# One queue less in front of the decays: loads of a recurrent attention, moved to another engine and to a later slot

## The chip, the cores and the metric

The program runs on one core of a Trainium2 chip. The metric is the device time of one execution in microseconds (us). The core has TensorE (PE: matrix products), VectorE (DVE), ScalarE (ACT), GpSimd (POOL) and SyncE (SP), each of which works through its own instructions in order. Transfers are issued by an instruction on one of these engines and are then carried out by 16 shared DMA engines; an instruction that needs a transfer's data waits on a semaphore. A queue in this text is the row of instructions of one engine, with the transfers that it issues.

## The reference, cut to what matters

Three stages follow each other: a recurrent attention (4 batches, 8 heads, 768 steps, head size 40), a mixture of experts with top-1 gating, and a second network with an ELU.

```python
for t in range(S):
    y[:, :, t] = np.einsum('bhd,bhde->bhe', rt, state)
    Sa = np.einsum('bhde,bhe->bhd', state, at)
    state_decay = state * wt[:, :, None, :] - np.einsum('bhd,bhe->bhde', Sa, bt)
    state = state_decay + np.einsum('bhd,bhe->bhde', vt, kt)
...
out[i] = gate_w[i] * y[expert_idx[i], pos[i]]      # per token: one of 8 experts, relu in between
...
return (g @ w_out).astype(np.float32)              # g = elu(x @ w_in)
```

## The kernel before, in words

The 768 steps are cut into 12 chunks of 64, and each chunk into two halves of the batch and head pairs: 24 units, each of 64 steps for 16 pairs. A chunk is computed with products instead of a loop over steps. For each unit the kernel needs the decays (with `a`, `k` and `b` in the same array, `e_in`), from which VectorE makes running products (`pre_dve`, L227 on); score matrices between steps (`scores`, L259); the inverse of a triangular 64x64 matrix per pair; and then a short serial part that uses the state that the unit two before has left (`rhs`, `u_solve`, `vu_tr`, `s_update`, `y_mm`, `x_out`).

The inverse is made in three steps. The scores of a unit are stored to DRAM (`dab`, L278) and loaded again in another layout (`lm_load`, L308). GpSimd then inverts all 32x32 diagonal blocks of a group of four units in one long row of small operations (`solve`, L319) and stores the result to DRAM (`dx`, `x_store`, L342). `tt_load` (L354) loads a unit's share of it into `TA` and `TT`, and `t64` (L409) joins the 32x32 blocks to 64x64: first a transpose on VectorE (L413), then products on TensorE (L420, L431). Groups of four start at units 4, 8, 12, 16 and 20 (units 0 to 3 have two groups of two).

The order of all work is written out by hand. A long string, `ORDER`, sets the beginning. From slot 5 to slot 24, `slot(k)` (L53) writes a slot's steps as a string of keys, and each key runs one step, up to its next `yield`. In slot k the serial part of unit k runs beside the preparation of unit k + 8 (its scores) and k + 9 (its running products), so that a slot has work of several units. The letters that matter here: `c` scores, `m` their mask, `l` the load of scores for the solve, `i` a third of a solve, `o` the store of its result, `e` the load of the decays, `d` the load of `r` and `v` (`RVU`), `v` a load for `rhs` (`VS`), `t` the load of an inverse, `g` joining it, `r` the product `rhs` with which a slot begins on TensorE, `w` the transposes of `VU`, `p` and `a` the running products and copies made from the decays.

All loads and stores named above are issued by SyncE, in program order, except most stores of `dx` and the scattered rows of the output, which GpSimd issues. A transfer that has to wait, for its source or for its buffer, holds SyncE's queue until it can go. The decays have two buffers (`EI`, in tiles called `ring`): those of unit u + 2 overwrite those of unit u, once unit u's scores and transposed keys (`kb_tr`, L286) are made. From slot 14 on there are no decays left to load, and from slot 17 on VectorE also converts weights for the last stage.

Of the kernel before, what the change touches and what calls it, by code (L numbers as in the profile page):

```python
# [22 lines left out]
NU = 24  # L23
LOOK = 8

FU, KMU = 4, 8
GROUPS = [(u, 2) for u in range(0, FU, 2)] + [(u, 4) for u in range(FU, NU, 4)]
# [17 lines left out]
h4 x2 l8 g4 c12.1 k12.0 D1 h4 t5 q3.0 p13 w3 g4 g4 g4 s3 u4 x2 a13 l12 s3 z3 q3.0 u4 w4 w4 a13 q3.1 p13 i3 w4 g5 h5 y3  # L45
d5 x2 w4 y3 s3 s4 i3 k12.0 e14 t6 s4 s4 h5
"""
AHEAD = (17, 19, 20, 21, 22, 23)

CV0, CVN = 17, 7  # L50
# [2 lines left out]
def slot(k):  # L53
    L = []
    a = lambda x: L.extend(x.split())
    live, prev = k < NU, k >= 1
    nx, up = k + 1, k + 8
    ups = up < NU
    pair = k - 3 if k >= 3 and k % 2 else None
    work = {f - 5 + i: (g, i) for g, (f, n) in enumerate(GROUPS) for i in range(3) if n == 4 and f > 4}  # L60
    w = work.get(k)
    if k + 2 < NU: a(f"v{k+2}")
    if live: a(f"r{k} r{k}")
    if ups: a(f"c{up}.0")
    if FU <= k < NU: a(f"g{k} g{k}")
    if ups: a(f"m{up}.0 c{up}.0")
    more = ups and up + 1 < NU
    if more: a(f"p{up+1}")
    if k < 2: a(f"c{up}.1 m{up}.1 c{up}.1 c{up}.1 l{up}")
    if k == 1: a(f"q{k-1}.0 q{k-1}.0 q{k-1}.1 q{k-1}.1")  # L70
    if k >= 2: a(f"x{k-2} x{k-2} x{k-2}")
    if k == NU: a(f"b{NU-2}.1")
    if FU <= k < NU: a(f"g{k} g{k}")
    if w and w[1]:
        a(f"i{w[0]}")
        if w[1] == 2: a(f"o{w[0]}")
    if k >= 4 and k % 2 == 0: a(f"D{k-3}")
    if ups and k > 1:
        a(f"c{up}.1 m{up}.1 c{up}.1 c{up}.1")
        if more: a(f"p{up+1}")  # L80
        a(f"l{up}")
    V = (lambda: a("V")) if CV0 <= k < NU else (lambda: None)
    if k > 1: a(f"q{k-1}.0 q{k-1}.0")
    V()
    if w and not w[1]: a(f"i{w[0]}")
    if live: a(f"u{k} u{k}")
    if more: a(f"p{up+1}")
    if k > 1: a(f"q{k-1}.1 q{k-1}.1")
    V()
    if 2 <= nx < NU: a(f"h{nx} h{nx}")  # L90
    if pair is not None: a(f"b{pair}")
    if ups:
        a(f"k{up}.0 k{up}.0 k{up}.1 k{up}.1")
        if up + 2 < NU: a(f"e{up+2}")
    if FU <= nx < NU: a(f"g{nx}")
    if live and k < 22: a(f"w{k} w{k} w{k} w{k}")
    if more: a(f"a{up+1} a{up+1}")
    if prev and k > 2: a(f"z{k-1}")
    if nx < NU: a(f"d{nx}")
    if k + 2 < NU: a(f"t{k+2}")  # L100
    if live and k < 22: a(f"s{k} s{k} s{k}")
    if k == NU: a(f"j{NU-2}.1 j{NU-2}.1 D{NU-2}")
    if prev: a(f"y{k-1} y{k-1}")
    V()
    if pair is not None: a(f"j{pair} j{pair} D{pair}")
    return " ".join(L)


def attention(tc, nc, e_in, v_tok, d_in, wg, disp, cst, ring, early, cv, cap):
# [8 lines left out]
    def bank(nm):  # L118
        return ps.tile([128, 512], F32, tag="ps", name=nm)
# [90 lines left out]
    def q64(t):  # L210
        return t.rearrange("p (q t) -> p q t", t=65)[:, :, 0:64]

    def load_e(u, half=None):
        c = slice(0, 2058) if half is None else slice(1034 * half, 1034 + 1024 * half)
        t = EI[u % 2]
        for hp in range(2):
            nc.sync.dma_start(out=t[64 * hp:64 * hp + 40, c], in_=e_in[u, hp, :, c])

    def load_v(u):
        VS = VSs[u % 3]  # L220
# [286 lines left out]
    def q_mm(u, g):  # L507
        V, R = VUt[u % 2], Rbd[u % 2]
        p = bank("q")
        for i in range(4):  # L510
            h = 4 * g + i
            nc.tensor.matmul(p[:, 128 * i:128 * i + 128], V[:, h].rearrange("p x t -> p (x t)"), R[:, h], start=True, stop=True)  # L512
        yield
        if ("Qs", u) not in st:
            st["Qs", u] = wk.tile([128, 8, 2, 64], F32, tag="Qs", name="Qs", bufs=1)
        Qs, m = st["Qs", u], mask.unsqueeze(1).to_broadcast([128, 8, 64])
        nc.vector.tensor_tensor(Qs[:, 4 * g:4 * g + 4].rearrange("p h b t -> p (h b) t"), p.rearrange("p (l t) -> p l t", t=64), m, op=ALU.mult)
# [86 lines left out]
    def zero_d(e):  # L604
        zero(disp[e * NTOK:e * NTOK + 512, :])

    steps = dict(sz=set_z, se=set_e, sa=set_a, sd=set_d, sv=set_v, st=set_t, sr=set_r, ss=set_s, sx=set_x, sw=set_w, sc=set_c, lw=load_w,
                 e=load_e, v=load_v, d=load_d, p=pre_dve, a=pre_act, c=scores, m=am_evac, k=kb_tr, l=lm_load, i=solve, o=x_store,
                 n=m_load, t=tt_load, f=t32, g=t64, r=rhs, u=u_solve, w=vu_tr, s=s_update, h=s_tr, q=q_mm, z=y_state, y=y_mm, x=x_out,
                 b=route, j=route_mm, D=scatter, Z=zero_d, V=lambda: cv.pieces(spare, CVN))  # L610

# [12 lines left out]
    def go(key):  # L624

        if key not in open_:
            nm = key.rstrip("0123456789.")
            args = map(int, key[len(nm):].split(".")) if nm != key else ()
            open_[key] = part(steps[nm], args)
        next(open_[key], None)  # L630
# [10 lines left out]
    for k in range(KR, NU + 1):  # L641
        for key in slot(k).split():
            go(key)
        for _ in range(AHEAD.count(k)):
            next(early, None)
        if 8 <= k < 14:
            i = k - 8
            zero(cst["yd"][4096 + 512 * i:4608 + 512 * i, :])
# [65 lines left out]
class Ring:  # L714
# [8 lines left out]
    def next(s, split):  # L723
        k = s.turn[split]
        s.turn[split] += 1
        return [s.tile(i, F32R) for i in ((1, 2), (4, 5), (6, 7), (8, 9))[k % 4]] if split else s.tile((0, 3)[k % 2], F32)
# [505 lines left out]
def network(tc, nc, e_in, v_tok, d_in, wg, cap, w1, w2, w_in, w_out, out):  # L1232
    with tc.tile_pool(name="cst", bufs=1) as p, tc.tile_pool(name="dsp", bufs=1, space=DRAM) as dp, tc.manual_schedule():
        cst = consts(p)
        disp = dp.tile([8 * NTOK, D], F32, name="disp")
        cst["yd"] = dp.tile([4096 + NTOK, D], F32, name="yd")
        ring = Ring(p)
        w32 = dp.tile([4, 128, 2816], F32, name="w32")
        W0, cv = expert(nc, ring, w1, w2, 0), Convert(nc, w_in, w_out, w32)
        attention(tc, nc, e_in, v_tok, d_in, wg, disp, cst, ring, ahead(W0), cv, cap)  # L1240
        ffn(tc, nc, cst, disp, w1, w2, w32, out, ring, W0, cv)
# [26 lines left out]
```

## Time and profile before

| | us |
|---|---|
| median of 3 runs | 1132.35 (1128.07 to 1134.58) |
| the profiled execution | 1126.71 |
| its span, first to last instruction | 1125.0 |
| TensorE busy in it | 996.1 (89%) |
| VectorE busy | 739.7 (66%) |
| GpSimd busy | 575.2 (51%) |
| ScalarE busy | 500.3 (44%) |

The attention takes up to about 464 us of the span, the two networks the rest. Times in rows are counted from the start of the span, so that a row at 213.58 lies in the attention. Slots are named by the k of `slot(k)`; in the profile slot 7 begins at 194.62 us, slot 8 at 207.89 and slot 20 at 393.0, each time with the `rhs` product. The mean granted TensorE clock over the whole span is 0.922 of full speed.

### The profile page before, as it was taken

Reading aid. Unit: us, or ns where it says so; the run is one execution under the profiler, and the core shown is the slowest. Engines: PE = TensorE matmul, PEld = TensorE weight load, DVE = VectorE, ACT = ScalarE, POOL = GpSimd, SP = SyncE. Lnnn points to the kernel's source line nnn. Section 1 sums busy time; section 2 is a strip of 40 time slices with the busy share of each in tenths; the row PEclk is TensorE's granted clock in tenths of the full one; section 3 lists DMA queues with packets and bytes.
Section 4 is the critical chain, followed back from the end, with each engine's and each line's share of the span. In section 5 each row is a group of like instructions: output and inputs, shape, how many; then the busy total and the mean of one; then the engine's idle time right before and its main releaser. Section 6 shows DMA issues by size and latency. Waiting matters only on the chain.

```text
span 1125.0 us, 25504 instructions
## 1 busy us (share of the span) xinstructions
PE 996.1 (89%) x10287; PEld 901.0 (80%) x10287; DVE 739.7 (66%) x1234; ACT 500.3 (44%) x968; POOL 575.2 (51%) x671
## 2 busy tenths in 40 slices
PE   4868888799899889679999999979999999999991
PEld 4767888798798878578888889858988989899891
DVE  8767557577674756478888882257775757575651
ACT  4655445455463333324333334435555555555540
POOL 4759559495886822435434445553443434353331
PEclk8878788889899889689999999989999999999996
DMA  6677674566765564666767744310100101010001
GB/s 173 161 182 198 169 128 104 122 148 174 173 148 139 146 157 116 172 175 164 216 197 214 207 139 155 136 55 6 28 21 8 40 7 42 1 47 1 24 1 31
DMA packets 189216, 127.26 MB, mean 113 GB/s; under 512 B 102776, under 2 KB 177016, under 8 KB 187448
## 3 DMA queue, kind: packets, MB, share of 16 engines
q1 hardware_dynamic: 185912, 114.42, 39.7%
q0 software_dynamic: 3168, 11.03, 3.1%
q8 instruction: 85, 1.39, 0.5%
q14 instruction: 51, 0.42, 0.1%
HBM read 87.39 MB, written 38.03 MB: 111 GB/s over the span
## 4 chain that ended last, share of the span: by engine, by line
PE 62%; DVE 13%; DMA 9%; POOL 6%; issue 5%; SPq 2%; ACT 2%; POOLq 0%; DVEq 0%; ACTq 0%
PE ph L922 21%; PE po L938 7%; PE po L937 7%; PE po L936 7%; DMA ring<-in_e_in_dram 3%; PE q L512 3%; PE sc L264 3%; POOL ring L338 2%; POOL X L340 2%; PE y L526 2%; DVE N L829 2%; PE x L549 2%; PE ut L456 2%; PE rhs L446 1%; PE st L481 1%
## 5 line engine op out<-in xcount | busy, mean ns | idle before, releaser
L965 POOL TENSOR_TENSOR L<-E,H 128x512 fp32r<-128x512 f32 x91 | 122.0, 1341 | 197.8 <-ACT H L964 193.0
L745 POOL TENSOR_TENSOR ring<-ring,ring 128x704 fp32r<-128x704 f32 x80 | 142.7, 1798 | 156.0 <-ACT ring L744 155.4
L938 PE MATMUL po<-ring,L 128*128 128x320 f32 x640 | 199.9, 312 | 14.7 <-DVE L L951 13.4
L936 PE MATMUL po<-ring,H 128*128 128x320 f32 x640 | 198.2, 310 | 0.8 <-ACT H L964 0.7
L937 PE MATMUL po<-ring,H 128*128 128x320 f32 x640 | 198.0, 309 | 0.0
L922 PE MATMUL ph<-XH,ring 128*128 128x512 f32 x640 | 182.8, 408 | 0.5 <-ACT XH L912 0.5
L938 PEld LDWEIGHTS po<-ring,L 128*128 128x128 f32 x640 | 120.7, 189 | 19.5 <-DVE L L951 17.5
L922 PEld LDWEIGHTS ph<-XH,ring 128*128 128x128 f32 x640 | 114.6, 192 | 17.7 <-ACT XH L912 1.9
L936 PEld LDWEIGHTS po<-ring,H 128*128 128x128 f32 x640 | 120.6, 188 | 9.0 <-ACT H L964 2.2
L937 PEld LDWEIGHTS po<-ring,H 128*128 128x128 f32 x640 | 120.6, 188 | 7.1
L958 ACT ACTIVATE E<-N 128x512 f32<-128x512 f32 x96 | 60.7, 633 | 139.9 <-POOL L L965 73.1
L340 POOL TENSOR_TENSOR X<-X,ring 128x60 f32<-128x60 f32 (+19 forms) x170 | 109.2, 642 | 13.3
L957 DVE TENSOR_SCALAR N<-ph 128x512 f32<-128x512 f32 x96 | 66.1, 689 | 72.6 <-PE ph L922 69.4
L922 PE MATMUL ph<-XL,ring 128*128 128x512 f32 x320 | 101.8, 399 | 0.0
L922 PE MATMUL ph<-XS,ring 128*128 128x512 f32 x320 | 101.2, 397 | 0.0
L338 POOL TENSOR_TENSOR ring<-X,ring 128x60 f32<-128x60 f32 (+19 forms) x108 | 70.8, 656 | 47.6 <-DMA ring<-dab 39.7
L962 DVE SCALAR_TENSOR_TENSOR M<-E,M 128x512 f32<-128x512 f32 x96 | 89.6, 933 | 0.2 <-ACT M L959 0.2
L264 PE MATMUL sc<-ring,ring 128*128 128x128 f32 x384 | 66.1, 330 | 17.6 <-ACT ring L251 11.0
L264 PEld LDWEIGHTS sc<-ring,ring 128*128 128x128 f32 x384 | 58.6, 235 | 19.3 <-ACT ring L251 11.0
L922 PEld LDWEIGHTS ph<-XL,ring 128*128 128x128 f32 x320 | 61.1, 191 | 15.1
L963 DVE SCALAR_TENSOR_TENSOR E<-ph,M 128x512 f32<-128x512 f32 x96 | 66.4, 691 | 9.9 <-DVE M L962 0.5
L922 PEld LDWEIGHTS ph<-XS,ring 128*128 128x128 f32 x320 | 60.6, 189 | 15.0
(222 smaller groups left out, 1867.9 us busy)
## 6 DMA issues: line engine op xcount, KB each, us to landing
ring<-in_w_dram SPq DMA_DIRECT2D x16, 640.0 KB
ring<-in_e_in_dram SPq DMA_DIRECT2D x28, 321.6 KB
ring<-in_w_dram SPq DMA_DIRECT2D x32, 256.0 KB
RVU<-in_d_in_dram SPq DMA_DIRECT2D x48, 160.0 KB
dab<-AB SPq DMA_DIRECT2D x24, 256.0 KB
ring<-w SPq DMA_DIRECT2D x4, 1408.0 KB
disp<-ring SPq DMA_DIRECT2D x8, 640.0 KB
X<-disp SPq DMA_DIRECT2D x7, 640.0 KB
```

The costliest lines, as they stand in the source:

```text
L264: nc.tensor.matmul(p[:, 128 * i:128 * i + 128], kb[:, q].rearrange("p x t -> p (x t)"), A[:, :, q, :], start=True, stop=True)
L338: nc.gpsimd.tensor_tensor(tv, X[:, 0:n, s:s + 1].to_broadcast([128, n, m]), N[:, s:s + 1, s + 1:e].to_broadcast([128, n, m]), op=ALU.mult)
L340: nc.gpsimd.tensor_tensor(X[:, 0:n, s + 1:e], X[:, 0:n, s + 1:e], tv, op=ALU.subtract)
L745: s.nc.gpsimd.tensor_tensor(s.L[g][:, c], R[:, c], s.H[g][:, c].bitcast(F32), op=ALU.subtract)
L922: nc.tensor.matmul(p, l, r, start=i == 0, stop=i == len(seq) - 1)
L936: nc.tensor.matmul(o, H[:, c], hb, start=f == 0, stop=False)
L937: nc.tensor.matmul(o, H[:, c], lb, start=False, stop=False)
L938: nc.tensor.matmul(o, L[:, c], hb, start=False, stop=last)
L957: nc.vector.tensor_scalar(N, p, 0.0, None, op0=ALU.min)
L962: nc.vector.scalar_tensor_tensor(out=M, in0=E, scalar=1.0, in1=M, op0=ALU.add, op1=ALU.mult)
L963: nc.vector.scalar_tensor_tensor(out=E, in0=p, scalar=0.0, in1=M, op0=ALU.max, op1=ALU.add)
L965: eng.tensor_tensor(L, E, H.bitcast(F32), op=ALU.subtract)
```

## The change

Two moves, both in `slot(k)`. First, the load of the decays is issued by ScalarE instead of SyncE (`E` instead of `e`), in slots 5 to 13, which load units 15 to 23; it stands behind the copies of `w`. Second, for the first unit of the groups at 8, 12, 16 and 20 (`FIRST`), the load of the inverse (`t`) moves from slot k - 2 of that unit to the middle of slot k - 1, ahead of that slot's `d` and behind its `c` and `l`, and the transpose with which `g` begins moves from the middle to the end of slot k - 1. No transfer and no operation is added or removed.

```diff
+FIRST = [f for f, n in GROUPS if f > 6]
...
     V = (lambda: a("V")) if CV0 <= k < NU else (lambda: None)
+
+    if nx in FIRST: a(f"t{nx}")
     if k > 1: a(f"q{k-1}.0 q{k-1}.0")
...
     if ups:
         a(f"k{up}.0 k{up}.0 k{up}.1 k{up}.1")
-        if up + 2 < NU: a(f"e{up+2}")
-    if FU <= nx < NU: a(f"g{nx}")
+    if FU <= nx < NU and nx not in FIRST: a(f"g{nx}")
     if live and k < 22: a(f"w{k} w{k} w{k} w{k}")
+    if up + 2 < NU: a(f"E{up+2}")
     if more: a(f"a{up+1} a{up+1}")
     if prev and k > 2: a(f"z{k-1}")
     if nx < NU: a(f"d{nx}")
-    if k + 2 < NU: a(f"t{k+2}")
+    if k + 2 < NU and k + 2 not in FIRST: a(f"t{k+2}")
     if live and k < 22: a(f"s{k} s{k} s{k}")
     if k == NU: a(f"j{NU-2}.1 j{NU-2}.1 D{NU-2}")
     if prev: a(f"y{k-1} y{k-1}")
+    if nx in FIRST: a(f"g{nx}")
...
-    def load_e(u, half=None):
+    def load_e(u, half=None, eng=nc.sync):
...
-            nc.sync.dma_start(out=t[64 * hp:64 * hp + 40, c], in_=e_in[u, hp, :, c])
+            eng.dma_start(out=t[64 * hp:64 * hp + 40, c], in_=e_in[u, hp, :, c])
...
+                 e=load_e, E=lambda u: load_e(u, eng=nc.scalar), v=load_v, d=load_d, p=pre_dve, a=pre_act, c=scores, m=am_evac, k=kb_tr, l=lm_load, i=solve, o=x_store,
```

Lines after the change stand 3 or 4 further down, so a `TA<-dx` load is L366 before and L370 after. SyncE's queue from slot 6's score store on, before: `ring<-in_e_in` are the decays (unit 16, then 17), `dx_2199` the inverses of group 8.

```order
L278 DMA dab_2442<-AB 64x1024
L317 DMA ring_102<-dab_2442 16x32x32 x2
L217 DMA ring_99<-in_e_in_dram 40x2058 x2
L225 DMA RVU_128<-in_d_in_dram 40x16x64
L225 DMA RVU_128<-in_d_in_dram 40x8x128
L366 DMA TA<-dx_2199 32x16x32
L367 DMA TA<-dab_1174 32x16x32
L372 DMA TT_131<-dx_2199 32x8x32 x4
L221 DMA VS_146<-in_v_tok_dram 64x640
L278 DMA dab_2656<-AB 64x1024
L317 DMA ring_102<-dab_2656 16x32x32 x2
L217 DMA ring_100<-in_e_in_dram 40x2058 x2
```

The same place after the change:

```order
L282 DMA dab_2442<-AB 64x1024
L321 DMA ring_102<-dab_2442 16x32x32 x2
L229 DMA RVU_128<-in_d_in_dram 40x16x64
L229 DMA RVU_128<-in_d_in_dram 40x8x128
L225 DMA VS_146<-in_v_tok_dram 64x640
L282 DMA dab_2649<-AB 64x1024
L321 DMA ring_102<-dab_2649 16x32x32 x2
L370 DMA TA<-dx_2199 32x16x32
L371 DMA TA<-dab_1174 32x16x32
L376 DMA TT_131<-dx_2199 32x8x32 x4
L229 DMA RVU_127<-in_d_in_dram 40x16x64
L229 DMA RVU_127<-in_d_in_dram 40x8x128
```

The decays have left the queue, and the six loads of unit 8's inverse stand behind slot 7's score store and load instead of ahead of them, with unit 8's `RVU` loads behind them. ScalarE in slot 6 after the change (the copies of `VU` are `w`, those of `ring` and `AM` are `a`; before, the row with the load is not there):

```order
L299 COPY KB_121<-kbt 128x320 x2
L474 COPY VU<-vu 128x320 x2
L221 DMA ring_99<-in_e_in_dram 40x2058 x2
L255 COPY ring_101<-ring_100 64x512
L257 COPY AM_143<-ring_100 64x8x64
L255 COPY ring_101<-ring_100 64x512
L257 COPY AM_143<-ring_100 64x8x64
L499 COPY VS_148<-S0E_136 64x8x40
```

Four copies for the next slot's scores now stand behind the two issues. VectorE at the end of slot 7, before (`AB<-TA` is the transpose of unit 8's inverse, `XT` the scaled output of unit 6):

```order
L413 STREAM_TRANSPOSE AB<-TA 32x512
L490 TENSOR_TENSOR S0E_134<-st,S0E_135 104x8x40
L491 TENSOR_TENSOR S0E_134<-S0E_134,ring_102 104x8x40
L493 COPY VS_146<-S0E_134 64x8x40
L543 TENSOR_TENSOR XT<-y,GE_109 104x512
```

And after:

```order
L494 TENSOR_TENSOR S0E_134<-st,S0E_135 104x8x40
L495 TENSOR_TENSOR S0E_134<-S0E_134,ring_102 104x8x40
L497 COPY VS_146<-S0E_134 64x8x40
L547 TENSOR_TENSOR XT<-y,GE_109 104x512
L417 STREAM_TRANSPOSE AB<-TA 32x512
```

The transpose has moved behind the update of the state and behind `XT`. TensorE and GpSimd have the same instructions in the same order as before.

## Rows read from the trace of the kernel before

**Rows 1.** The page's chain that ended last: shares of the span by engine.

```profile
PE 62%; DVE 13%; DMA 9%; POOL 6%; issue 5%; SPq 2%; ACT 2%; POOLq 0%; DVEq 0%; ACTq 0%
```

**Rows 2.** Windows of slots 7, 8, 14, 20: length, engines' busy us, clock, DMA.

```profile
194.62:207.89 13.27, 13.27 (x273) 12.52 (x270) 10.89 (x23) 8.54 (x20) 7.60 (x15) 1.00 0.52 134
207.89:231.22 23.33, 16.16 (x276) 14.84 (x276) 10.78 (x22) 8.63 (x19) 13.19 (x22) 0.78 0.55 116
...
314.96:328.35 13.39, 13.39 (x277) 12.65 (x276) 12.11 (x22) 8.25 (x19) 12.12 (x16) 1.00 0.72 168
...
393.00:412.00 19.00, 13.97 (x246) 13.05 (x246) 9.59 (x23) 5.22 (x12) 4.98 (x5) 0.73 0.67 180
```

**Rows 3.** Timeline of SyncE's queue in slots 6 and 7: start, us, instruction.

```profile
191.77 0.73 SPq L217 DMA_DIRECT2D ring<-in_e_in_dram  x2
192.80 1.69 SPq L225 DMA_DIRECT2D RVU<-in_d_in_dram  x2
203.13 0.34 SPq L366 DMA_DIRECT2D TA<-dx  x1
...
208.97 0.54 SPq L278 DMA_DIRECT2D dab<-AB  x1
212.63 0.84 SPq L317 DMA_DIRECT2D ring<-dab  x2
213.58 0.73 SPq L217 DMA_DIRECT2D ring<-in_e_in_dram  x2
```

**Rows 4.** SyncE's waits: total us, times, the longest.

```profile
SPq L366 <- DMA dx<-X: 34.3, 4, 13.3
```

**Rows 5.** Timeline of ScalarE in slot 7.

```profile
202.44 0.58 ACT L268 COPY AB<-sc 64x512 f32<-64x512 f32 x1 [2.68 <-DVE AM L282]
...
204.59 0.75 ACT L470 COPY VU<-vu 128x320 f32<-128x320 f32 x2
...
206.64 0.62 ACT L251 COPY ring<-ring 64x512 f32<-64x512 f32 x1
```

**Rows 6.** The chain that ended last, in slots 8 and 16: start, us, what.

```profile
208.97 3.65 DMA dab<-AB
213.99 6.28 DMA ring<-in_e_in_dram
...
345.76 4.34 DMA RVU<-in_d_in_dram
```

**Rows 7.** Timeline of VectorE: the scans of slots 7 and 8, and slot 19's `XT`.

```profile
198.61 1.34 DVE L230 TENSOR_TENSOR_SCAN ring<-ring,DR 104x520 f32<-104x520 f32 x1 [1.27 <-DMA ring<-in_e_in_dram]
...
220.36 1.25 DVE L230 TENSOR_TENSOR_SCAN ring<-ring,DR 104x520 f32<-104x520 f32 x1 [9.60 <-DMA ring<-in_e_in_dram]
...
399.50 0.69 DVE L543 TENSOR_TENSOR XT<-y,GE 104x512 f32<-104x512 f32 x1
```

**Rows 8.** Timeline of GpSimd: first operations of solves, stores of `dx`, the clearing.

```profile
216.38 0.23 POOL L338 TENSOR_TENSOR ring<-X,ring 128x31 f32<-128x31 f32 x1 [9.68 <-DMA ring<-dab]
...
266.70 0.62 POOL L346 DMA_DIRECT2D dx<-X  x1 [0.30 <-POOL X L340]
...
274.02 0.16 POOL L330 MEMSET X<- 128x32 f32 x1
282.80 0.23 POOL L338 TENSOR_TENSOR ring<-X,LM 128x31 f32<-128x31 f32 x1 [8.62 <-DMA LM<-dab]
...
332.43 0.61 POOL L346 DMA_DIRECT2D dx<-X  x1 [0.30 <-POOL X L340]
...
346.94 0.23 POOL L338 TENSOR_TENSOR ring<-X,ring 128x31 f32<-128x31 f32 x1 [8.01 <-DMA ring<-dab]
...
391.47 0.61 POOL L346 DMA_DIRECT2D dx<-X  x1 [0.30 <-DVE req L570]
```

**Rows 9.** Timeline of TensorE in slot 20: the product that joins unit 20's inverse.

```profile
398.41 1.06 PE L420 MATMUL xp<-AB,TA 32*32 32x32 f32 x32 [4.25 <-DMA TA<-dab]
```

**Rows 10.** The line that loads the decays: ns min/median/max of an issue on SyncE.

```profile
L217 SPq DMA_DIRECT2D ring<-in_e_in_dram x68: 281/325/2119, 2.1 to 312.7; - x68
```

More of the change, by code (lines that the diff above doesn't have):

```diff
@@ L607, in attention @@
     steps = dict(sz=set_z, se=set_e, sa=set_a, sd=set_d, sv=set_v, st=set_t, sr=set_r, ss=set_s, sx=set_x, sw=set_w, sc=set_c, lw=load_w,
-                 e=load_e, v=load_v, d=load_d, p=pre_dve, a=pre_act, c=scores, m=am_evac, k=kb_tr, l=lm_load, i=solve, o=x_store,
+                 e=load_e, E=lambda u: load_e(u, eng=nc.scalar), v=load_v, d=load_d, p=pre_dve, a=pre_act, c=scores, m=am_evac, k=kb_tr, l=lm_load, i=solve, o=x_store,
                  n=m_load, t=tt_load, f=t32, g=t64, r=rhs, u=u_solve, w=vu_tr, s=s_update, h=s_tr, q=q_mm, z=y_state, y=y_mm, x=x_out,
```

## The prediction

> **What bounds the kernel now.** I read the page's chain first. Most of it is TensorE [rows 1], but DMA, POOL and issue hold a fifth, so there are stretches in which TensorE waits. The change touches only slots 5 to 19 of the attention; the MoE half of the program, from about 464 us on, only moves along. I therefore cut the attention at the starts of its slots (each begins with the `rhs` product) and asked for the busy time of each [rows 2]. Slots 7 and 14 last 13.27 and 13.39 us, and TensorE is busy in all of it at full clock: that is the floor. Slots 8 and 20 last 23.33 and 19.00 us. In slot 8 the same products also take 16.16 us instead of 13.3: the granted clock is 0.78 on average there, so it falls to the lower of its two levels (1.2 instead of 2.4 GHz) after the idle time. Slots 7 to 14 together take 328.35 - 194.62 = 133.7 us, 16.7 on average, against a floor of 13.3.
>
> Next, why. SyncE's queue is served in order. In slot 6 it reaches the load of the first inverse of group 8 (`TA<-dx`), whose source POOL is still computing, and stands there: behind the two `RVU` loads (1.69 us from 192.80) the queue is free at 194.49, and `TA<-dx` starts at 203.13 [rows 3]. That is 8.6 us. Four such waits sum to 34.3 us, the longest 13.3 [rows 4]. Behind it stand slot 7's own score store (`dab<-AB`, 208.97), `ring<-dab` (212.63) and the decay load `ring<-e` (213.58). The score had been copied at 203.02 and the buffer of the decays was free at 205.34, when the last `VU<-vu` copy ended, since the products that read it come before that copy [rows 5]. The decays land at 220.27 [rows 6], VectorE's scan has waited 9.60 us for them, against 1.27 in slot 7 [rows 7], and slot 8 is 10 us over the floor. So one late inverse holds back decays that need nothing from it.
>
> The second loop is POOL. It solves one group in 216.38 to 266.70 (50.3 us to the store of the result), is ready for the next at 274.18, and then waits 8.62 us for the last scores of that group, which stand in SyncE's same queue; before the solves at 216.38 and 346.94 it waited 9.68 and 8.01 [rows 8]. The last solve ends the stage: its store at 391.47 releases the inverse on which the product at 398.41 has waited 4.25 us [rows 8, 9]. So a gain before 347 us counts only as far as it starts POOL's solves earlier.
>
> **The change, part by part.** (a) The decay loads of units 15 to 23 (nine pairs) leave SyncE for ScalarE, behind the second `VU<-vu` copy. In slot 7 that is 205.34 instead of 213.58. In an undisturbed slot it is no gain: in slot 6 SyncE issued at 191.77, 2.85 us before slot 7 began [rows 2, 3]; ScalarE would issue 2.55 us before the slot's end (207.89 - 205.34) [rows 2, 5]. I charge 0.3 us to each such slot.
>
> (b) ScalarE pays the issue of two loads in each of nine slots. The trace has no load issued there. From below it is nothing; from above 2 x 2.12, the longest issue of such a load on SyncE; the median there is 0.325, and POOL's issue of a store takes 0.62 [rows 8, 10]. I take the median, 0.65 a slot. Behind it stand the `ring<-ring` copies, which the next slot's score product reads: the second ends at 206.64 + 0.62 = 207.26 [rows 5], the product comes after `rhs`, about 1.1 us after 207.89 [rows 2], so 1.7 us of cover hide it. Without the cover all 0.65 would be on the path. The loads also wait for an earlier ScalarE copy and for a transfer of the slot before; both have ended when ScalarE gets there, so I add no wait.
>
> (c) The decays are no longer alone in SyncE's queue ahead of `RVU`: they run beside `ring<-dab` and `RVU`. Bounds: no loss, or all of an `RVU` load (4.34 us from issue to landing [rows 6]) in front of them. `RVU` follows the scores, which in an undisturbed slot are issued about when the decays are, so most of the decays should be ahead. I take 0.6 us, nearer the lower end. With (a) a slot with decays becomes 13.3 + 0.3 + 0.6 = 14.2 us.
>
> (d) The inverse load of units 8, 12, 16, 20 is asked for one slot later, ahead of that slot's `RVU` load and behind its scores. It adds no transfer, but its six issues now stand before `RVU`: from the first of them to the next store it was 5.8 us in slot 6 (203.13 to 208.97 [rows 3]). `RVU` is needed just before the `VU<-vu` copies, 10.0 us into the next slot (204.59 - 194.62 [rows 2, 5]), so this is covered unless the inverse is some 3 us late. VectorE's transpose of it moves behind the `XT` product of the slot, so the product that waits is only the one that uses the inverse. In slot 19 `XT` ran at 399.50, behind that transpose, when TensorE already stood in slot 20 at the product that needs the inverse [rows 2, 7, 9]; having it done beforehand is worth 1 us.
>
> **The sum, forward from slot 7** (194.62, taken unchanged). Slot 8 begins at 208.8. Slot 7's scores are copied 0.9 later than before, 203.9, and their store goes at once: 3.65 us to landing [rows 6], then 3.75 from `ring<-dab` to the solve (212.63 to 216.38): POOL starts group 12 at 211.3, 5.1 earlier. It stores after 50.3, at 261.6, and is ready 7.5 later, at 269.1. Slot 11 begins at 208.8 + 3 x 14.2 + 0.5 (slot 8's inverse lands a little late) = 251.9; its scores are with POOL 16.7 us into the slot (9.3 + 3.65 + 3.75), 268.6. So group 16 starts at 269.1 rather than 282.80 and stores 49.6 later (332.43 - 282.80), at 318.7; ready 7.5 later, 326.2. Slot 15 begins at 251.9 + 4 x 14.2 = 308.7, its scores arrive at 325. Group 20 starts at 326.2, not 346.94: 20.7 us earlier, and its store comes 20.7 earlier, as the solve keeps its 44.5 us. TensorE by itself reaches slot 20 at 308.7 + 64.7 (slot 15 began at 328.35 and slot 20 at 393.0 [rows 2]) = 373.4, 19.6 earlier, and needs the inverse 5 us or less later; it comes at about 377. So both loops meet near 20.7. With the 1 us of (d), and 1 us taken off because POOL's solves run beside a denser VectorE (50.3 us beside the scans, 44.5 without), 20.7 stays. The profiled execution takes 1126.71 with its surroundings, so 1106.0; the median of the runs shown is 1132.35, 5.6 above it, and it is the median that is forecast: 1111.6, rounded to 1111.
>
> **Rules that speak against it.** In the trace the decays waited behind another load's wait, not for issue time [rows 3]. The Trainium skill (DMA: Bandwidth & Descriptors, "Issuing engines are not separate DMA queues") says that loads from several engines share the same 16 DMA engines and that spreading them saves only the issue time. By that rule 9 x 0.65 = 5.9 us of SyncE's time would be all; it does not speak of a wait at the head of a queue. The same page ("Queues, rings and completion order") says that a DMA engine takes turns between the queues that have work, which bears on (c); no row of this kernel shows two such queues side by side.
>
> **Rivals.**
> 1. ScalarE pays more for the issue, or the decays land a little later: a slot of 15.3. Then slot 11 begins at 256, POOL gets its scores at 272.8 and 330.8 instead of being ready first, and the gain is 346.94 - 330.8 = 16, less 1 to 2: 1118. For it: ScalarE has 1.7 us of cover and the longest issue is 2.12; against: the median. At 16.0 a slot it would be 1124.
> 2. The wait only moves. POOL still ends late, and TensorE stands at the inverse in the slot that needs it, as at 398.41. For it: POOL's 50.3 + 7.5 is already 57.8 of the 66.4 us between two solves. Against: 8 to 10 us of waiting for scores before each solve are in the same queue and go. If POOL's operations stretch beside a denser VectorE by these 8 us, nothing is left but 2 to 3: 1129.
> 3. Slower: the `RVU` and score loads go ahead of the decays in every slot, all 4.34 us. The scan is then 4.6 us late and a slot lasts 17.9, against 16.7 before: nine slots lose 1.2 each, and the transposes no longer have a gap to wait in: 1142. It decides from a delay of 3.4 us a slot (16.7 - 13.3) on. Against it: ScalarE asks about as early as SyncE asks for the scores.
> 4. Better than forecast: slots at the floor and fewer clock drops, and the sixth slot shortened too (its decays were also late): 1101.
>
> **Numbers.** Forecast 0.55 (its own range 1105 to 1115), rival 1 0.22, rival 2 0.10, rival 3 0.08, rival 4 0.05. A change under 0.5% (5.7 us) can't be told from none: faster is under 1126.7, so 0.55 + 0.22 + 0.05 = 0.82; the same 0.10; slower 0.08. The range leaves out rival 3, part of 2 and the best of 4: 1101 to 1129.
>
> **What would show it.** SyncE's waits for `dx` at group 8 should be gone, at 12 to 16 under 3 us, and stay long at 20. Decays issued 0 to 1 us after the last `VU<-vu` copy and landed 6 to 7.5 us later; slots 7 to 14 of 14 to 15 us, clock near 1.00. POOL's waits before the solves of groups 12, 16 and 20 should fall from 9.7, 8.6, 8.0 to 5, 1, 1, and the last store come near 370. Wrong if `ring<-ring` copies or the score product wait behind the issue on ScalarE (rival 1), if slots stay at 16 to 17 with the scan waiting for decays (rival 3), or if POOL's solves grow past 53 us (rival 2).

## The result: 1119.29 us, 1.1% faster, and the profile after

| | before | after |
|---|---|---|
| median of 4 runs each, side by side | 1132.06 us (1128.07 to 1134.58) | 1119.29 us (1118.48 to 1120.68) |
| ratio, 95% interval | | 0.9892 [0.9861, 0.9923] |
| the profiled execution, its span | 1126.71, 1125.0 | 1120.68, 1119.0 |
| mean granted TensorE clock | 0.922 | 0.929 |

The kernel became faster by 12.8 us; 21 had been forecast. The two profiled executions differ by only 6.0: that of before is quicker than all of its timed runs, that of after the slowest of its own. So the traces below can place only some 6 us of the gain, and the verdict rests on the medians. A second comparison of the two kernels gave 0.9892 [0.9873, 0.9911].

Lines moved by three or four: the decays' loads are L221, the loads of the inverse L370, its store L350, its transpose L417, the product that uses it L424, the scatter of output rows L600.

The same windows as in [rows 2], cut at the `rhs` products of slots 7, 8, 16 and 20 of the kernel after, and last all of slots 7 to 14 (from and to, length, busy us of PE, PEld, DVE, ACT and POOL, granted clock, DMA share, GB/s):

```profile
193.56:206.93 13.37, 13.37 (x277) 12.62 (x273) 10.67 (x22) 8.64 (x21) 11.67 (x17) 1.00 0.54 126
206.93:230.12 23.19, 16.46 (x270) 15.64 (x270) 11.22 (x23) 8.44 (x20) 14.31 (x23) 0.78 0.62 129
336.71:353.84 17.13, 13.27 (x246) 12.44 (x246) 5.47 (x15) 4.55 (x11) 13.45 (x27) 0.80 0.36 72
393.28:406.13 12.85, 12.03 (x246) 11.34 (x246) 8.78 (x22) 5.22 (x12) 3.62 (x3) 0.87 0.71 184
193.56:322.57 129.01, 115.31 (x2158) 108.72 (x2156) 92.56 (x173) 68.92 (x154) 104.11 (x136) 0.92 0.70 160
```

Slot 20 fell from 19.00 to 12.85 us, its clock from 0.73 up to 0.87. Slot 8, which the change was to shorten most, did not move: 23.19 for 23.33, at the same clock of 0.78. Slot 16, also the first of its group, grew from 12.32 us (341.54 to 353.86 before) to 17.13: TensorE waits there 1.82 and 2.03 us for loads that its inverse needs. The eight slots from 7 to 14 take 129.0 us, against 133.7 before and 114 forecast (194.62 to 308.7).

The wait at the head of SyncE's queue is half gone. SyncE's waits for the store of the inverse: total us, times, the longest. [rows 4] had 34.3, 4, 13.3:

```profile
SPq L370 <- DMA dx<-X: 17.9, 4, 6.5
```

The decays go out where the change meant them to. ScalarE in slots 6 and 7 (start, us, queue or line, what; in brackets the idle time before it):

```profile
190.94 0.67 ACTq L221 DMA_DIRECT2D ring<-in_e_in_dram  x2
191.71 0.62 ACT L255 COPY ring<-ring 64x512 f32<-64x512 f32 x1 [0.38 <-ACT VU L474]
...
204.07 0.71 ACTq L221 DMA_DIRECT2D ring<-in_e_in_dram  x2
```

In slot 6 the issue of two loads lasts 0.67 us and 0.38 of it shows as a gap in front of the next copy; over the nine slots it lasts 0.67 to 1.66 us, 0.73 at the median. Slot 7's decays leave at 204.07 instead of 213.58 [rows 3].

What waits in slot 8 instead is seen in the chain that ended last, slots 6 to 8 and 11 (start, us, what):

```profile
191.32 6.42 DMA ring<-in_e_in_dram
...
205.31 7.70 DMA dx<-X
...
274.32 5.67 DMA TA<-dx
```

Slot 6's decays need 6.42 us, about as before (6.28 [rows 6]). But the store of the inverse (`dx<-X`), which GpSimd issues 1.2 us behind slot 7's decays, now needs 7.70. Before, the same store of group 8 was issued at 199.16 and released `TA<-dx` at 203.13 [rows 3], 3.97 us later:

```profile
199.16 0.61 POOL L346 DMA_DIRECT2D dx<-X  x1 [0.30 <-POOL X L340]
```

In the kernel after it also leaves 6.15 us later, at 205.31. The loads of the inverse stand in SyncE's queue behind the load of slot 7's scores, and behind that SyncE was free from 206.81 on:

```profile
205.04 1.77 SPq L321 DMA_DIRECT2D ring<-dab  x2
```

What ran beside the store is seen when the time from its issue to its landing is cut out as a window, after and then before (columns as above):

```profile
205.31:213.01 7.70, 3.94 (x96) 3.60 (x92) 2.22 (x5) 2.72 (x6) 1.64 (x2) 0.99 0.76 183
```

```profile
199.16:203.13 3.97, 3.97 (x59) 3.78 (x58) 3.87 (x8) 1.24 (x4) 1.64 (x2) 1.00 0.50 183
```

The DMA engines moved 183 GB/s in both. The store and a scatter are 0.69 MB in either window. What the window of after has besides, by DMA queue (packets, MB, share of the 16 engines' time): `q10` carries the decays alone (the kernel before has no such queue), `q1` is here the load of scores, `ring<-dab`.

```profile
q10 hardware_dynamic: 90, 0.58, 29.6%
q1 hardware_dynamic: 1056, 0.13, 14.8%
```

Which of the two slows the store, the experiments below tell. Over the four stores of 512 KB the median to landing is 4.7 us, 3.9 before.

TensorE stands at the product with the inverse, and VectorE at its transpose, instead of at the scan [rows 7]. First TensorE, then VectorE's transpose and the scan behind it, all in slot 8 (in slot 12 TensorE waits 3.79 us):

```profile
215.98 1.06 PE L424 MATMUL xp<-AB,TA 32*32 32x32 f32 x32 [6.73 <-DMA TA<-dab]
```

```profile
214.91 0.70 DVE L417 STREAM_TRANSPOSE AB<-TA 32x512 f32<-32x512 f32 x1 [6.59 <-DMA TA<-dx]
216.90 1.22 DVE L234 TENSOR_TENSOR_SCAN ring<-ring,DR 104x520 f32<-104x520 f32 x1
```

The scan that had waited 9.60 us for decays does not wait at 216.90. The transpose just ahead of it has waited 6.59.

GpSimd, to be laid beside [rows 8]: stores of the inverse, a scatter behind the first of them, the first operation of the next solve.

```profile
205.31 0.61 POOL L350 DMA_DIRECT2D dx<-X  x1 [0.30 <-DVE roh L577]
...
214.47 0.96 POOL L600 DMA_INDIRECT disp<-XO,SLOT  x1 [7.21 <-DMA disp<-XO,SLOT]
...
216.75 1.41 POOL L342 TENSOR_TENSOR ring<-X,ring 128x31 f32<-128x31 f32 x1
...
271.04 0.62 POOL L350 DMA_DIRECT2D dx<-X  x1 [0.30 <-DVE ACC L580]
...
281.66 1.59 POOL L342 TENSOR_TENSOR ring<-X,LM 128x31 f32<-128x31 f32 x1
...
332.42 0.61 POOL L350 DMA_DIRECT2D dx<-X  x1 [0.30 <-POOL X L344]
...
340.63 0.23 POOL L342 TENSOR_TENSOR ring<-X,ring 128x31 f32<-128x31 f32 x1
...
383.87 0.61 POOL L350 DMA_DIRECT2D dx<-X  x1 [0.30 <-POOL X L344]
```

None of these solves waits for scores any more (9.68, 8.62 and 8.01 before). Yet the solve of group 12 starts at 216.75 and not earlier than before (216.38): the store of group 8 left 6.15 us later, and behind it the second of two scatters has waited 7.21 us for the first, which runs beside the decays. Group 16 starts 1.1 us earlier than before, group 20 6.3, and the last store comes 7.6 earlier.

Two solves also became longer. From the first operation to the store, that of group 8 took 49.9 us (155.39 to 205.31) and not 45.4 (153.78 to 199.16), that of group 12 54.3 and not 50.3. The reason shows at single operations: one that runs beside a scan or a multiply of VectorE's running products takes 0.6 to 1.2 us longer. The same operation near the end of group 12's solve, before, and then after with the scan beside it:

```profile
263.25 0.37 POOL L338 TENSOR_TENSOR ring<-X,ring 128x112 f32<-128x112 f32 x1
```

```profile
264.66 1.18 POOL L342 TENSOR_TENSOR ring<-X,ring 128x112 f32<-128x112 f32 x1
```

```profile
264.34 1.34 DVE L239 TENSOR_TENSOR_SCAN GE<-ring,ring 104x520 f32<-104x520 f32 x1
```

Each unit has four such operations on VectorE. The solve of group 12 had those of three units beside it before and has those of four now, as they start earlier and follow each other more closely; in the solve of group 8 they rose from 9 to 13.

### The profile page after: what moved, and what is told of

Its sections match the earlier page's. It is cut to its first block, busy times and chain, and to the rows that moved or that the text cites. A ratio compares the mean times of both kernels' runs of the same rounds, so it can differ in the third digit from the quotient of the medians.

```text
span 1119.0 us, 25504 instructions
## 1 busy us (share of the span) xinstructions
PE 990.8 (89%) x10287; PEld 896.9 (80%) x10287; DVE 737.5 (66%) x1234; ACT 500.4 (45%) x968; POOL 585.5 (52%) x671
## 4 chain that ended last, share of the span: by engine, by line
PE 62%; DVE 12%; DMA 9%; POOL 5%; issue 5%; SPq 3%; ACT 2%; DVEq 0%; POOLq 0%; ACTq 0%
PE ph L926 21%; PE po L942 7%; PE po L941 7%; PE po L940 7%; PE q L516 3%; PE sc L268 2%; POOL ring L342 2%; DMA ring<-in_e_in_dram 2%; PE ut L460 2%; PE x L553 2%; POOL X L344 2%; DMA ring<-in_w_dram 2%; PE y L530 1%; PE t L435 1%; DVE N L833 1%
## 5 line engine op out<-in xcount | busy, mean ns | idle before, releaser
L942 PE MATMUL po<-ring,L 128*128 128x320 f32 x640 | 199.7, 312 | 14.7 <-DVE L L955 13.5
L344 POOL TENSOR_TENSOR X<-X,ring 128x60 f32<-128x60 f32 (+19 forms) x170 | 113.6, 668 | 13.3
L342 POOL TENSOR_TENSOR ring<-X,ring 128x60 f32<-128x60 f32 (+19 forms) x108 | 76.3, 706 | 29.3 <-DMA ring<-dab 21.0
L926 PEld LDWEIGHTS ph<-XS,ring 128*128 128x128 f32 x320 | 60.3, 189 | 15.3 <-DVE XS L917 0.5
```

What stands on the lines that cost most here:

```text
L342: nc.gpsimd.tensor_tensor(tv, X[:, 0:n, s:s + 1].to_broadcast([128, n, m]), N[:, s:s + 1, s + 1:e].to_broadcast([128, n, m]), op=ALU.mult)
L344: nc.gpsimd.tensor_tensor(X[:, 0:n, s + 1:e], X[:, 0:n, s + 1:e], tv, op=ALU.subtract)
L926: nc.tensor.matmul(p, l, r, start=i == 0, stop=i == len(seq) - 1)
L942: nc.tensor.matmul(o, L[:, c], hb, start=False, stop=last)
```

## The experiments

The theory behind them: the whole gain comes from the inverse being asked for later; the decays, moved to ScalarE, run in slots 7 and 11 beside the store of the inverse, its loads and the scatters, and cost part of it again. The rivals: the decays' move is what pays; the store is late because of GpSimd's queue and not because of the decays; or GpSimd is not what sets the end. All ratios are to runs of the kernel before on the same chip.

**Only the decays on ScalarE** (the inverse asked for where it was before):

```
-        if up + 2 < NU: a(f"e{up+2}")
 ...
+    if up + 2 < NU: a(f"E{up+2}")
```

> Only the decays move to ScalarE's queue; the inverse of the first unit of a group is asked for where it was before, two slots ahead. Theory A (the scores of the next solve are what had to be freed, because GpSimd's chain of solves sets the end): SyncE still stands at dx in slots 6, 10, 14 and 18, so the score stores behind it are as late as before, GpSimd starts its solves at about 216, 283 and 347 us as before, and the time is within 4 us of before (ratio 0.996 to 1.000). Theory B (the late decays were the whole loss, and asking later for the inverse only moves a wait): nearly all of the gain is here, ratio 0.988 to 0.991.

Measured: 1138.37 us, ratio 1.0053 [1.0033, 1.0073], slower than before, and outside what either theory expected. The wait at the head of SyncE's queue is still there:

```profile
SPq L368 <- DMA dx<-X: 49.4, 4, 15.6
```

On ScalarE the decays do not escape it. In slots 7 and 11 ScalarE's queue stands some 8 us at their issue until loads of the inverse (`TT<-dx`) have landed, and the copies for the next score product stand behind it. ScalarE and TensorE in slots 7 and 8:

```profile
208.97 1.14 ACTq L219 DMA_DIRECT2D ring<-in_e_in_dram  x2
210.20 0.62 ACT L253 COPY ring<-ring 64x512 f32<-64x512 f32 x1 [8.64 <-DMA TT<-dx]
```

```profile
212.14 2.08 PE L266 MATMUL sc<-ring,ring 128*128 128x128 f32 x8 [6.79 <-ACT ring L253]
```

So slot 7's decays leave at 208.97 and not at 204.07 as in the kernel after, and those of slot 11 at 281.40, later than before (280.68). Why their issue waits for loads that it does not use is not shown. The scores of slot 11 go out beside the decays. SyncE's queue, ScalarE's issue beside it, GpSimd's solve that waits, and the chain in the slot behind:

```profile
282.15 1.60 SPq L280 DMA_DIRECT2D dab<-AB  x1
289.83 0.84 SPq L319 DMA_DIRECT2D LM<-dab  x2
```

```profile
281.40 0.70 ACTq L219 DMA_DIRECT2D ring<-in_e_in_dram  x2
```

```profile
293.43 0.63 POOL L340 TENSOR_TENSOR ring<-X,LM 128x31 f32<-128x31 f32 x1 [13.52 <-DMA LM<-dab]
```

```profile
298.03 8.89 DMA ring<-in_e_in_dram
```

The store of scores, issued 0.75 us behind the decays, has landed 7.7 us later, where it took 3.65 before [rows 6], and GpSimd waits 13.52 us for these scores, not 8.62. So the moved loads gain nothing while the wait stays. What decays that leave early are worth, this kernel cannot say; that their delay is not what the time hangs on, the next one shows.

**Only the inverse later** (the decays stay on SyncE, in slots 7 and 11 now behind the loads of the inverse):

```
+    if nx in FIRST: a(f"t{nx}")
 ...
-    if k + 2 < NU: a(f"t{k+2}")
+    if k + 2 < NU and k + 2 not in FIRST: a(f"t{k+2}")
 ...
+    if nx in FIRST: a(f"g{nx}")
```

> Only the inverse of the first unit of a group is asked for one slot later, and its transpose moves; the decays stay in SyncE's queue, in slots 7 and 11 now behind that wait. Theory A: the scores go ahead of the wait, GpSimd starts its solves nearly as early as in the changed kernel, and half or more of the gain is kept although the scans of slots 8 and 12 wait some 6 us for their decays: ratio 0.990 to 0.995. Theory B: the decays wait at dx as before, so no gain, ratio 0.998 to 1.004.

Measured: 1119.69 us, ratio 0.9888 [0.987, 0.9906]. This is the whole gain of the change (0.9892), without the decays on ScalarE, and a little more than the 0.990 to 0.995 expected of the first theory. SyncE's issue of slot 7's decays, and the scan that waits for them:

```profile
213.87 0.72 SPq L221 DMA_DIRECT2D ring<-in_e_in_dram  x2
```

```profile
220.41 1.33 DVE L234 TENSOR_TENSOR_SCAN ring<-ring,DR 104x520 f32<-104x520 f32 x1 [5.85 <-DMA ring<-in_e_in_dram]
```

These decays leave as late as before (213.58 [rows 3]), and the gain is there all the same. The solves of groups 12, 16 and 20 start at 214.24, 280.48 and 343.16, 2 to 4 us earlier than before. So the moved wait pays; the moved loads, taken together, add nothing to it.

**The kernel after, with the store of the inverse issued by SyncE directly ahead of its loads**:

```
-        eng = nc.sync if g == 2 else nc.gpsimd
+        eng = nc.sync if g >= 2 else nc.gpsimd
```

> The changed kernel, but the results of the solves of groups 8 to 20 are stored by SyncE, directly ahead of the load that needs them, instead of by GpSimd behind the solve. In the changed kernel the store at 205.31 took 7.70 us to land, beside the decays issued at 204.07; before it took 3.9 at the median. Theory C (the slow landing belongs to GpSimd's own queue): the store lands in about 3 to 4 us, each group's first inverse comes 3 to 4 us earlier and GpSimd can clear its tile earlier, 6 to 12 us less than the changed kernel, ratio 0.979 to 0.984. Theory D (the slow landing is the decays on the same DMA engines): it still takes 6 to 8 us, and the time is that of the changed kernel within 3 us, ratio 0.987 to 0.992.

Measured: 1124.93 us, ratio 0.9929 [0.9911, 0.9946], a little over the 0.987 to 0.992 expected if the decays are the cause: SyncE comes to the store of group 16 only at 335.84, 6 us after its solve has ended (329.78). The chain and SyncE's queue:

```profile
204.33 6.75 DMA dx<-X
211.16 1.89 DMA TA<-dx
...
268.85 7.87 DMA dx<-X
```

```profile
335.84 0.44 SPq L350 DMA_DIRECT2D dx<-X  x1
338.87 0.30 SPq L370 DMA_DIRECT2D TA<-dx  x1
```

Out of SyncE's queue the store takes 6.75 and 7.87 us where decays have just been issued, and 3.03 (335.84 to 338.87) where there are none; with the decays over, the load behind it takes 1.89, not 5.67. GpSimd's queue is not the cause; the decays beside the store are, as the next kernel shows.

**The kernel after, with the decays of slots 7 and 11 alone back on SyncE, behind the loads of the inverse**:

```
-    if up + 2 < NU: a(f"E{up+2}")
+    if up + 2 < NU: a(f"{'e' if nx in FIRST else 'E'}{up+2}")
```

> The changed kernel, but in slots 7 and 11 the decays are issued by SyncE behind the loads of the inverse, so that nothing of them is in flight while the result of the solve is stored and loaded. Theory D: the store lands in 3 to 4 us and the loads of the inverse in under 3, so the inverse comes 4 to 6 us earlier; the decays of these two slots come some 10 us later, and the two effects about cancel: ratio 0.986 to 0.993. Theory C: the store still takes 6 to 8 us, the decays are later all the same, and the time is 4 to 10 us over the changed kernel, ratio 0.993 to 0.998.

Measured: 1114.03 us, ratio 0.9844 [0.9818, 0.987], better than the 0.986 to 0.993 expected. The chain, and the scores' load during the first store (205.82 to 210.23):

```profile
205.82 4.41 DMA dx<-X
...
269.12 3.85 DMA dx<-X
```

```profile
q1 hardware_dynamic: 1035, 0.13, 18.9%
```

The store takes 4.41 and 3.85 us again, with the load of scores beside it as in the kernel after: of the two, it is the decays that slow it. From these stores to the next solve GpSimd needs 8.12 and 8.58 us (205.82 to 213.94, 269.12 to 277.70), where the kernel after needs 11.44 and 10.62. The last store of the inverse comes at 380.55 instead of 383.87. By these ratios, the decays on ScalarE gain 0.44% in the plain slots (0.9844 against 0.9888) and cost 0.48% in these two (0.9892 against 0.9844). The intervals are about as wide as that, and the 0.9892 comes from other runs, so the next kernel tests the sum, and three kernels side by side at the end test the distance itself.

**The reverse of it**: decays on ScalarE only in slots 7 and 11.

```
-    if up + 2 < NU: a(f"E{up+2}")
+    if up + 2 < NU: a(f"{'E' if nx in FIRST else 'e'}{up+2}")
```

> The inverse is asked for one slot later, as in the changed kernel, and the decays go out from ScalarE in the two slots of each four in which the inverse is solved and loaded (slots 7 and 11), from SyncE in all others. Additive theory (the effects of the decays in these slots and in the plain ones add up): 0.9888 (the inverse's move alone) and +0.0048 (what the decays on ScalarE cost there, 0.9892 against 0.9844) give 0.9936, some 1125 us. Rival (the cost appears only once the plain slots are shorter): as the inverse's move alone, 0.989, some 1119.5 us.

Measured: 1121.0 us, ratio 0.9934 [0.9904, 0.9965]. The additive theory's 0.9936 lies inside the interval, and 0.989 just outside. But the quotient of the medians is 0.991 (1121.0 by 1130.79), and 1121.0 us is nearer to the rival's 1119.5 than to 1125: whether the two effects add up is not decided. The trace shows the effect on the store once more, in two kernels that differ in these decays alone, here and in the kernel with only the inverse later:

```profile
204.52 7.40 DMA dx<-X
```

```profile
206.14 4.44 DMA dx<-X
```

**More work for GpSimd** (the kernel after, eight unread multiplies behind each solve):

```
+        if g >= 4:
+            for _ in range(8):
+                nc.gpsimd.tensor_tensor(tmpT[:, 0:256], st["XB", g][:, 0:256], ..., op=ALU.mult)
```

> The changed kernel, with eight more 128x256 multiplies on GpSimd at the end of each of the solves of groups 12, 16 and 20, whose results nobody reads. If GpSimd's chain of solves sets the end of this stretch, the time rises by nearly all that they take, by an estimate 14 to 16 us: some 1134 us (ratio 1.002). If TensorE or the decays set it and GpSimd has slack, it rises by under 5 us (ratio under 0.9935).

Measured: 1129.86 us, ratio 0.9998 [0.9972, 1.0023]. The groups of the added line (busy us, mean ns of one) and the last store of the inverse:

```profile
L347 POOL TENSOR_TENSOR ring<-X,ring 128x256 f32<-128x256 f32 x16 | 13.0, 815 | 1.3
L347 POOL TENSOR_TENSOR ring<-X,LM 128x256 f32<-128x256 f32 x8 | 5.9, 737 | 0.6
```

```profile
401.52 0.61 POOL L353 DMA_DIRECT2D dx<-X  x1
```

18.9 us were added (13.0 + 5.9), the last store came 17.65 later (401.52 for 383.87), and the time rose by 1.06%, 12.0 us (against the kernel after in other runs): two thirds, a little under the 14 to 16 expected and far over 5. So GpSimd's chain sets most of the end of this stretch in the kernel after.

**Solves in four parts**, on top of the kernel with the decays of slots 7 and 11 behind the inverse:

```
-            if s and s % 12 == 0 and e == 32:
+            if s and s % (8 if g >= 4 else 12) == 0 and e == 32:
```

> As the changed kernel with the decays of slots 7 and 11 issued by SyncE behind the inverse's loads (1114.0 us), and the solves of the groups from 12 on cut in four parts instead of three, so that no two of the scatters stand directly behind each other on GpSimd. If the waits of the scatters for what stands before them (3.9 to 4.6 us at each solve) are time of the path, some 2 us of each of the three groups come free: 1108 to 1110 us. If the clearing of the tile behind the inverse's store holds GpSimd anyway, or another engine sets the end, no change: 1113 to 1115 us.

Measured: 1112.64 us, ratio 0.9864 [0.9825, 0.9902]: of the two expectations nearer to no change (1113 to 1115) than to 1108 to 1110. The waits of the scatters are gone; between the store and the clearing GpSimd now waits only for the store to land, here behind group 12:

```profile
265.74 0.61 POOL L350 DMA_DIRECT2D dx<-X  x1 [0.30 <-POOL X L344]
...
269.49 0.95 POOL L333 MEMSET X<- 128x1024 f32 x1 [1.82 <-DMA dx<-X]
```

**The same with two tiles for the inverse**, so that the clearing need not wait for the store:

```
-    LM2 = one.tile([128, 32, 32], F32, name="LM2")
+    X5 = one.tile([128, 1024], F32, name="X5")
 ...
-            t = st["XB", g] = X4[:, 0:1024]
+            t = st["XB", g] = X5 if g % 2 else X4[:, 0:1024]
```

> As the kernel with solves in four parts, and two tiles for the inverse in turn instead of one (a third mask buffer is given up for it), so that the clearing of the tile does not wait until the store of the inverse has landed. If GpSimd sets the end, the store's landing (3.9 to 4.5 us for each group) comes free as well: 1102 to 1106 us. If TensorE's slots set it by then, 1108 to 1114 us; if the mask buffers were needed, above 1114 us.

Measured: 1112.2 us, ratio 0.9866 [0.9825, 0.9906]: no further gain, and the 1102 to 1106 expected of a GpSimd that still sets the end is missed; it lies in the 1108 to 1114 expected if TensorE's slots set the end by then. In these two traces the last store of the inverse comes at 375.2 and 375.9, five us before 380.55, and the time does not follow. That is weak evidence: the second trace of the kernel of 380.55, from the runs below, has this store at 376.84.

**Three of these side by side once more**, on one chip: the kernel after, the one with the decays of slots 7 and 11 behind the inverse, and the latter with solves in four parts.

> The changed kernel once more, beside the next two on one chip, since their distances (0.3 to 0.5%) are no larger than the intervals of runs on different chips. If the earlier ratios hold: 0.989.

> The changed kernel with the decays of slots 7 and 11 issued by SyncE behind the inverse's loads, once more. If the store and the loads of the inverse are really slowed by the decays beside them: 0.0035 to 0.006 below the changed kernel of this call, some 0.984 to 0.985. If the earlier distance was chance: within 0.002 of it.

> The kernel before this one with solves in four parts, once more. If GpSimd's chain still sets the end there, 0.0015 to 0.003 below it (the store of the last inverse came 5.3 us earlier in the trace); if TensorE's slots set it by then, within 0.0015 of it.

Measured: 1117.31, 1112.96 and 1110.54 us; ratios 0.9892 [0.9873, 0.9911], 0.9863 [0.9844, 0.9882] and 0.9844 [0.9824, 0.9863]. The decays behind the inverse gain 0.29% on the kernel after (0.39% by the medians, 0.48% in the earlier runs): of one sign each time, by the ratio a little under the 0.35 to 0.6% expected of a real effect and over the 0.2% allowed to chance, with intervals that overlap a little. The solves in four parts are 0.2% ahead here, as expected if GpSimd still sets the end, and 0.2% behind in the earlier figures, which came from two chips: whether they gain anything stays open. Both beat the kernel before by 1.4 to 1.6% and the kernel after by 0.3 to 0.5%.

## Why the prediction was right in kind and too large

**What bounds the kernel** held. The late inverse at the head of SyncE's queue was the cost; taking only this wait away gives 0.9888. That the decays were what suffered from it did not hold as a reason for the gain: with decays as late as before (213.87) the whole gain is there. They were the visible wait. That the scores behind the same wait were the ones that counted fits the solves, which start 2 to 4 us earlier then; no run moves the scores alone.

**Parts (a) and (b)** held in the main. The issue takes 0.67 to 1.66 us per slot, 0.73 at the median (0.65 forecast). Slots 9, 10 and 13, which load decays and stand behind no late inverse, last 14.0, 13.7 and 14.5 us (14.2 forecast).

**Part (c)** is the first step that failed. It asked what sharing does to the decays: 0.6 us, bounded by one `RVU` load. Slot 6's decays lose 0.1 (6.42 for 6.28); those of slot 7 were landed before anyone asked, as the scan at 216.90 did not wait. It did not ask what they do to the transfers beside them, which are on the path of GpSimd and of TensorE: in slot 7 the store of the inverse takes 7.70 instead of 3.97 and the second scatter waits 7.21 for the first; in slot 11, where the store left 0.9 us ahead of the decays (271.04 and 271.94) and took 3.28, the load of the inverse takes 5.67. The Trainium skill (DMA: Bandwidth & Descriptors, "Queues, rings and completion order") says that a DMA engine takes turns between the queues that have work; the lengthened store agrees with it, also in that it does not matter whether GpSimd or SyncE issues it (7.70, 6.75).

**Part (d)** half held. SyncE's wait is shorter and VectorE's early transpose is gone, but the inverse was later than the 3 us for which cover was claimed: TensorE stood 6.73 us at it in slot 8, and the clock of that slot stayed at 0.78. Two delays meet there. SyncE was free for the load at 206.81. Had only the store's landing grown, it would have been there by 206.9 (199.16 + 7.70); had only the solve become late, by 209.3 (205.31 + 3.97); with both it was 213.0.

**The sum** can be followed row by row on GpSimd. Forecast: ready 7.5 us after each store; measured 11.44 (205.31 to 216.75), 10.62 (271.04 to 281.66) and 8.21 (332.42 to 340.63), together 7.8 more. Some 5.4 of it are the decays', by the 8.12 and 8.58 us in the kernel without them beside the store. Forecast: solves of 50.3, 49.6 and 44.5; measured 54.3, 50.8 and 43.2, together 3.9 more. And the solve of group 8, taken as unchanged, stored at 205.31, so that with 7.5 group 12 would have started at 212.8 instead of 211.3: 1.5 more. 7.8 + 3.9 + 1.5 = 13.2, and the last store came at 383.87 instead of 370.8 (391.47 - 20.7), 13.1 late. The execution was forecast at 1106.0 and took 1120.68, 14.7 more. The 13 us are therefore nearly the whole miss in the profiled execution.

**The length of the solves** is the second step that failed. The sum took 1 us off for a denser VectorE; the solve of group 12 alone lost 4.0. Its length goes with the units whose running products fall into it: 50.3 or 50.4 us with three (before, only the inverse later, decays on ScalarE only in slots 7 and 11), 54.3 to 55.2 with four (two traces each of the kernel after and of the one with the decays behind the inverse), and 53.1 with three and a half (only the decays on ScalarE). So VectorE's running products, coming earlier and closer together, lengthened the solve beside them.

The offset failed too: 5.6 us were added because the median of before lies that far over its profiled execution. After, the median lies 1.4 below.

**The rivals.** The forecast of 1118 (rival 1) came nearest in time, but not by its mechanism: ScalarE's issue and the slots were about as cheap as expected. Nor does its row come out of its own slots: 256 + 4 x 15.3 + 16.7 is 333.9, not 330.8, which would have made it some 1121. Rival 2, "the wait only moves", describes slots 8 and 12, where TensorE waits at the inverse. Its reason, GpSimd's operations stretched beside a denser VectorE, came true at about half of its 8 us (4.5 and 4.0 for the solves of groups 8 and 12), and its sign, a solve over 53 us, showed at group 12 (54.3). What it missed is the decays' share. Rival 3 did not come about in the kernel after, the decays were not delayed; its opposite did, the decays delayed the small transfers. Of the signs listed: waits for scores of 5, 1 and 1 us were none at all; SyncE's waits for `dx` went to a longest of 6.5, not gone; slots 7 to 14 lasted 13.2 to 23.2 us, not 14 to 15; and the last store came at 383.87, not near 370.

## What to carry to other kernels

When one queue is held up by a late transfer, move the late transfer, and look for everything behind it that feeds the slowest loop; the wait that is longest in the profile (here the scan's 9.60 us for decays) need not be the one that sets the time. When a large load goes to a second queue, price what it does to the stores and loads that start within its six microseconds, above all those on the path: here a pair of loads of 0.66 MB cost such a store 3.3 to 4.8 us. Where such a transfer is late anyway, issue the large load behind it, in the same queue. And when one engine's work gets denser, ask what it does to an engine that works beside it, here VectorE's running products to GpSimd's solve.

## What the runs showed of the hardware

- A pair of decay loads (643 KB) slows a transfer issued 0.7 to 2.7 us behind it from another queue to about twice its time: the store of the inverse (512 KB) from 3.0 to 4.4 us up to 6.75 to 7.87, the store of scores (256 KB) from 3.65 to 7.7. The rate is no fixed one: over the store's 7.70 us and over the 3.97 of before the DMA engines moved the same 183 GB/s, at busy shares of 0.76 and 0.50, but 221 over the 7.7 us of the scores.
- The decays are not spared everywhere: in the kernel that moved only them, where they go out in the same tenth of a microsecond as the scores (298.03 and 297.99, 314.88 and 314.91), the chain has two of 8.89 and 8.07 us.
- An issue of two such loads on ScalarE takes 0.67 to 1.66 us, 0.73 at the median, and can overlap the end of the copy before it; on SyncE 0.73 [rows 3].
- A GpSimd operation of the solve that took 0.37 us took 1.18 beside a scan on VectorE. With the running products of one unit more beside it, a solve of some 50 us became 4 us longer.
- The same product sequence ran in 13.4 us in slot 7 (granted clock 1.00) and in 16.5 in slot 8 (0.78, between 1.2 and 2.4 GHz over the slot), after an idle time of 6.73 us.
